# Loads and swaps paced by twos, another model of instruction fetches, and another order, in a planned one-core kernel

## The chip, the cores and the metric

The kernel runs on one core of one Trainium2 chip. Its time is device microseconds (us) of one execution. Before the change it takes 639.13 us, the median of three runs that lie between 637.85 and 642.98 us.

## The reference

Two residual blocks over x of 2048 rows and 512 columns, each modulated by a conditioning vector c. The first is a long convolution with a kernel K that is made from complex exponentials, the second a feed-forward layer with a squared ReLU.

```python
mod = (_silu(c) @ w_mod).reshape(c.shape[0], 6, 1, -1)
sa, ca, ga, sb, cb, gb = (mod[:, 0], ..., mod[:, 5])
h = _layernorm(x) * (1 + ca) + sa
x = x + ga * _A_ref(h, ...)          # K = Re sum_n C exp(dt A l) dt B, then FFT convolution, + u * Dskip
h = _layernorm(x) * (1 + cb) + sb
x = x + gb * _B_ref(h, ...)          # r = relu(h @ w1 + b1); r * r @ w2 + b2, F = 1792
```

## The kernel before, in words

The convolution is done with transforms written as matrix products, in float32. The 512 channels are cut into 8 chunks (letters A to H), and the work is made of **pieces**:

- **rows** (L657 to L667, letter r): each of 16 tiles of x is normalised, turned by PE (L661, L664) into a bank of PSUM, and copied by ACT (L667) into `big`. There are three such banks (`ps`), used in turn.
- **u pieces** (A to H): stage 1 of the transform (L701, copied by ACT at L703) and stage 2 (L711, copied at L735). The stage 1 of any chunk needs all 16 rows.
- **swap** (0 to 7): two DMAs within SBUF (L742) that exchange the two halves of the 128 partitions of a chunk's spectrum, 512 KB each.
- **K units**, 32 of them: POOL adds a phase (L795) and makes amplitudes (L815, L819), ACT takes the sines of the phase (L805 to L807), DVE multiplies (L829 to L832), PE sums (L839), and K goes through stage 1 as well (L701 from `ksb`).
- **products** (a to h): stage 2 of K, the product with the spectrum and the swapped spectrum (L849), the sums (L857) and a copy to `big` (L863).
- **l**: the late modulation, that is sb, cb and gb (L621, L687). **x**: tables of exponentials on ACT (L786). **w**: eight loads of w1 (L933).

Then comes the inverse transform (L1024) with the constants `i2c` (2 MB, L965) and x again (`xt`, L984 and L1040), the second normalisation, transposes (L1064), and the feed-forward layer: three products for each (L1115 to L1118 and L1149 to L1151), with high and low parts of w1 (L977, L996) and of w2 (loads L1084, parts L973 and L974).

`ORDER`, a string, says after which K unit each piece is recorded. It does not fix the order on the engines: `keep_order` does. It takes all recorded instructions in groups, their dependencies and a cost for each, plays the program with one queue for each engine, takes at each step the ready group with the longest way to the end (plus an offset from `HURRY`), and ties each group to the one before it on its engine. So what stands in a row on an engine is a result of that play, and every engine works strictly in that row. On SP the play takes, of the DMAs that are ready, the one recorded first.

The play counts the instructions that PE has taken, in portions (`PACKET`), and delays PE when a portion would come late behind queued DMAs. These delays change only which group the planner picks; the chip fetches its instructions as it does.

Each DMA on SP signals one of eight semaphores in turn, so that the ninth waits for the first. Otherwise SP issues a DMA as soon as its data and its destination are free.

## Time and profile before

| | us |
|---|---|
| median of three runs | 639.13 |
| the profiled execution's own time | 637.81 |
| its span, first to last instruction | 636.0 |
| PE busy | 590.5 |
| DVE, ACT, POOL busy | 371.0, 349.6, 297.4 |

The span is 1.8 us shorter than the time of the same execution, and that execution is 1.3 us below the median. PE is TensorE, DVE VectorE, ACT ScalarE, POOL GpSimd, SP the engine that only issues DMAs. A row of the timeline gives start, duration, engine, line, operation, names (out<-in), shape and count, and in brackets how long the engine was idle before and what ended that. A float32 product stands twice in the trace, so that 16 products of the order are x32 there. "issue" means that the profile shows nothing for which the engine waited. PEclk is the granted clock of PE, 1.00 in full. In a DMA row, q1 is the queue of SP's transfers and q8 that of PE's instruction fetches: packets, MB, share of 16 DMA engines' time.

### The profile page before, as it was taken

Reading aid. Unit: us, or ns where it says so; the run is one execution under the profiler, and the core shown is the slowest. Engines: PE = TensorE matmul, PEld = TensorE weight load, DVE = VectorE, ACT = ScalarE, POOL = GpSimd, SP = SyncE. Lnnn points to the kernel's source line nnn. Section 1 sums busy time; section 2 is a strip of 40 time slices with the busy share of each in tenths; the row PEclk is TensorE's granted clock in tenths of the full one; section 3 lists DMA queues with packets and bytes.
Section 4 is the critical chain, followed back from the end, with each engine's and each line's share of the span. In section 5 each row is a group of like instructions: output and inputs, shape, how many; then the busy total and the mean of one; then the engine's idle time right before and its main releaser. Section 6 shows DMA issues by size and latency. Waiting matters only on the chain.

```text
span 636.0 us, 21183 instructions
## 1 busy us (share of the span) xinstructions
PE 590.5 (93%) x9474; PEld 510.4 (80%) x9474; DVE 371.0 (58%) x652; ACT 349.6 (55%) x651; POOL 297.4 (47%) x247
## 2 busy tenths in 40 slices
PE   1697897999999999898989999999999999999995
PEld 1476797999998899897868888888888888888884
DVE  6886978899799688546655332533325332252223
ACT  5957899889987948362856432253323433222220
POOL 6499699999999987039958100010000100000000
PEclk9999999999999999899999999999999999999999
DMA  8942014022132403662333000100001000010001
GB/s 319 392 140 68 3 35 105 19 55 45 29 70 69 120 4 86 185 250 88 95 110 99 1 1 0 67 0 2 0 1 66 1 1 0 1 66 1 0 1 66
DMA packets 21707, 42.33 MB, mean 67 GB/s; under 512 B 3696, under 2 KB 9200, under 8 KB 20336
## 3 DMA queue, kind: packets, MB, share of 16 engines
q1 hardware_dynamic: 21184, 40.84, 21.0%
q8 instruction: 74, 1.21, 0.8%
q10 hardware_dynamic: 432, 0.14, 0.1%
q14 instruction: 17, 0.14, 0.1%
HBM read 28.39 MB, written 4.19 MB: 51 GB/s over the span
## 4 chain that ended last, share of the span: by engine, by line
PE 72%; ACT 9%; POOL 7%; DVE 5%; issue 4%; DMA 2%; DVEq 0%; SPq 0%; ACTq 0%; POOLq 0%
PE tg L1149 8%; PE tg L1151 8%; PE tg L1150 8%; PE ps L711 7%; PE ps L1115 6%; PE ps L701 6%; PE ps L1116 6%; PE ps L1118 6%; PE ps L857 6%; PE kg L839 3%; PE kg L1115 2%; PE kg L1116 2%; PE kg L1118 2%; PE tg L1024 1%; ACT xy L703 1%
## 5 line engine op out<-in xcount | busy, mean ns | idle before, releaser
L1135 ACT ACTIVATE xy<-ps,b1c 128x512 f32<-128x512 f32 x42 | 29.0, 690 | 126.2 <-PE ps L1118 126.2
L1137 DVE SCALAR_TENSOR_TENSOR ps<-ps,b1c,xy 128x512 f32<-128x512 f32 x42 | 31.8, 758 | 111.1 <-ACT xy L1135 111.1
L1060 POOL TENSOR_TENSOR big<-big,lo 128x512 f32<-128x512 f32 x12 | 15.7, 1306 | 151.8 <-DVE xy L1057 151.8
L711 PE MATMUL ps<-xy,t_sb 128*64 128x64 f32 x2048 | 67.4, 223 | 3.7 <-issue 2.5
L711 PEld LDWEIGHTS ps<-xy,t_sb 128*64 128x64 f32 x2048 | 63.9, 138 | 6.3 <-issue 3.0
L857 PE MATMUL ps<-e_sb,xy 128*64 128x128 f32 (+2 forms) x1152 | 64.2, 270 | 1.9 <-ACT xy L703 1.0
L857 PEld LDWEIGHTS ps<-e_sb,xy 128*64 128x64 f32 x1152 | 59.9, 142 | 3.6 <-ACT xy L703 1.4
L819 POOL TENSOR_TENSOR rtl<-tables 128x1024 f32<-128x1024 f32 x22 | 43.4, 1972 | 0.1
L703 ACT COPY xy<-ps 128x512 f32<-128x512 f32 x64 | 37.0, 598 | 7.7 <-PE ps L701 7.4
L849 DVE TENSOR_TENSOR xy<-ps,xy 128x512 f32<-128x512 f32 x64 | 39.9, 682 | 1.3 <-PE ps L711 1.1
L1115 PE MATMUL ps<-h0h,w1h 128*128 128x512 f32 (+1 forms) x96 | 36.0, 381 | 0.0
L795 POOL TENSOR_TENSOR rtl<-lo,big 128x1024 int32<-128x1024 int32 x16 | 34.3, 2145 | 3.1 <-ACT tg L807 2.5
L701 PE MATMUL ps<-d_sb,big 128*64 128x128 f32 x512 | 32.7, 275 | 2.9 <-ACT big L667 1.4
L701 PE MATMUL ps<-d_sb,ksb 128*64 128x128 f32 x512 | 34.3, 279 | 0.5 <-ACT xy L703 0.4
L863 DVE COPY big<-ps 128x256 f32<-128x256 f32 (+1 forms) x66 | 24.2, 407 | 18.0 <-PE ps L857 17.8
L795 POOL TENSOR_TENSOR llph<-lo,big 128x1024 int32<-128x1024 int32 x16 | 34.5, 2159 | 0.2 <-ACT tg L807 0.2
L701 PEld LDWEIGHTS ps<-d_sb,big 128*64 128x64 f32 x512 | 28.1, 137 | 4.3 <-ACT big L667 1.7
L1115 PE MATMUL ps<-h,w1h 128*128 128x512 f32 x80 | 31.4, 393 | 0.0
L1135 ACT ACTIVATE xy<-kg,b1c 128x512 f32<-128x512 f32 x14 | 9.7, 690 | 39.5 <-PE kg L1118 39.5
L1137 DVE SCALAR_TENSOR_TENSOR kg<-kg,b1c,xy 128x512 f32<-128x512 f32 x14 | 10.6, 756 | 34.0 <-ACT xy L1135 34.0
L701 PEld LDWEIGHTS ps<-d_sb,ksb 128*64 128x64 f32 x512 | 28.8, 140 | 1.6 <-ACT xy L703 0.7
L839 PE MATMUL kg<-rtl 128*32 128x64 f32 x1408 | 25.5, 221 | 4.3 <-issue 3.1
(287 smaller groups left out, 1606.7 us busy)
## 6 DMA issues: line engine op xcount, KB each, us to landing
xy<-xt SPq DMA_DIRECT2D x32, 256.0 KB, 5.5
xy<-xy SPq DMA_DIRECT2D x16, 512.0 KB, 6.0
xy<-w_mod SPq DMA_DIRECT2D x6, 1024.0 KB, 9.2
out_dram<-xy SPq DMA_DIRECT2D x16, 256.0 KB, 2.1
xy<-w SPq DMA_DIRECT2D x14, 256.0 KB, 2.7
raw<-w SPq DMA_DIRECT2D x6, 512.0 KB, 5.3
t_sb<-c_t SPq DMA_DIRECT2D x1, 2048.0 KB, 10.9
i2c<-c_i SPq DMA_DIRECT2D x1, 2048.0 KB, 9.9
```

Of the source, the lines that this page charges most:

```text
L701: nc.tensor.matmul(ps[64 * r : 64 * r + 64, 128 * i : 128 * i + 128], src[:, i], d1_sb[:, r], start=True, stop=True)
L711: nc.tensor.matmul(ps[64 * r : 64 * r + 64, 64 * i : 64 * i + 64].rearrange("p (h q t) -> p q h t", h=2, t=2), t2_sb[:, 8 * g + i, r], src ...
L795: nc.gpsimd.tensor_tensor(ph.rearrange("p d r (a b) -> p (d r) a b", a=4), bc(low_phase[:, us].rearrange("p d r b -> p (d r) b"), 2, 4), b ...
L819: nc.gpsimd.tensor_mul(am[:, 0, :, 32:96].rearrange("p d (v x) -> p d v x", v=2), bc(et[:, 256 + 8 * d0 : 384 + 8 * d0].rearrange("p (y a) ...
L839: nc.tensor.matmul(kps[32 * q : 32 * q + 32, d, :], am[:, r, 4 * q + d, 64:96], am[:, r, 4 * q + d, 0:64], start=(r == 0), stop=(r == 1))
L857: nc.tensor.matmul(ps[64 * m : 64 * m + 64], pairs(y)[:, g, i // 2, 64 * m : 64 * m + 64, i % 2], e1_sb[:, h].rearrange("p (r j) -> p r j" ...
L1115: pe.append(nc.tensor.matmul(ps, w1h[:, q, fs], hh[:, q, cols], start=(q == 0), stop=False))
L1116: pe.append(nc.tensor.matmul(ps, wl[:, q], hh[:, q, cols], start=False, stop=False))
L1118: pe.append(nc.tensor.matmul(ps, w1h[:, q, fs], hl[:, q, cols], start=False, stop=(q == 3)))
L1149: pe.append(nc.tensor.matmul(acc, r2l[:, ms], hi_, start=(t == 0), stop=False))
L1150: pe.append(nc.tensor.matmul(acc, r2h[:, ms], lo_, start=False, stop=False))
L1151: pe.append(nc.tensor.matmul(acc, r2h[:, ms], hi_, start=False, stop=(t == NF - 1)))
```

## The change

1. `paced_load` issues a DMA and remembers it. From the third on, each gets a wait on the landing of the one two places before it (`PACED = 2`, `tc.add_manual_dep` in `keep_order`). It takes the place of the plain issue for the swaps, the w1 loads, `i2c`, the 16 late loads of x and the 14 loads of w2. Both DMAs of one swap remain back to back.
2. `i2c` is loaded in four DMAs of 512 KB. It is recorded ahead of the `xt` loads, as before, and the chain of waits now keeps that order, which before gave way where `i2c` was not ready.
3. The planner's model of instruction fetches has other numbers.
4. `ORDER` and `HURRY` hold other values, and so the planner makes another order.

```diff
+PACED = 2
-HURRY = (176674, 61960, 2605, 274089, 54201, -67055, -175605, 69371)
+HURRY = (392742, 14341, 1606, 250122, 75315, -221787, -342862, -308)
...
-    "rrrrrrrrrrrrrrrrCABCBCBlCBCBACBBA.AA.CAABA.xx.0Caaaa.a.aD1aa..bDbbbEE.DD.bDD2bEb.b.cDDEcccc.cxcc"
+    "rrrrrrrrrxrrxrrrrrCABCBCBCCBCAABB.BCAA.AA.BAl0.aCaaaaa.a.D1..abbbbD2EEx.DDbbDD.E.Dbb.EcDcccc.ccF"
...
+def within(ins):
+    return not any("Dram" in type(a.bass_ap.tensor).__name__.title() for a in (*ins.ins, *ins.outs))
...
+    wait = mybir.DependencyInfo(mybir.DependencyClass.Sync, mybir.DependencyReason.DATA)
     for x, y in behind:
-        before[group[x]].add(group[y])
+        before[group[y.name]].add(group[x.name])
+        tc.add_manual_dep(y, x.name, wait, reason="pace")
...
-                    fetched = max(asked[0] + asked[1], min(behind_ns - 1800, asked[0] + 4300)) + 2350
-                asked = (max(t, fetched), 1100 if fetched > t else 600)
+                    fetched = max(asked[0] + asked[1], min(behind_ns, asked[0] + 4500)) + 2400
+                asked = (max(t, fetched), 1100 if fetched > t else 750)
...
-            queued.append((now, landed))
+            queued.append((now, landed + (-1000 if within(groups[g][0]) else -300)))
...
+    def paced_load(to, of):
+        ins = nc.sync.dma_start(to, of).ins
+        if len(paced) >= PACED:
+            behind.append((paced[-PACED], ins))
+        paced.append(ins)
...
-            nc.sync.dma_start(sw[64 * h : 64 * h + 64], xs[64 - 64 * h : 128 - 64 * h])
+            paced_load(sw[64 * h : 64 * h + 64], xs[64 - 64 * h : 128 - 64 * h])
...
-    nc.sync.dma_start(i2c, c_i2.rearrange("p (j r a) -> p j r a", j=64, r=2))
+    for j in range(0, 64, 16):
+        paced_load(i2c[:, j : j + 16], c_i2.rearrange("p (j r a) -> p j r a", j=64, r=2)[:, j : j + 16])
```

In the changed kernel the lines are shifted: L805 is L818, L667 is L680, L795 is L808, L701 is L714, L711 is L724, L839 is L852, L621 is L634, L687 is L700, and every paced load has the line of the helper, L591.

**ACT at the end of the rows.** L667/L680 are the last copies of the rows, L703/L716 the first copy of stage 1, L805/L818 the sine of a unit's phase and L806/L819 its absolute value; `llph` is the buffer of the second unit. Before:

```order
L535 ACTIVATE big_83<-big_83,magic 128x4x64
L544 ACTIVATE big_83<-big_83 128x4x64
L545 ACTIVATE big_83<-big_83 128x4x64
L667 COPY big_84<-ps_159 128x128x4
L536 ACTIVATE big_83<-big_83,magic 128x4x64
L537 ACTIVATE big_83<-big_83,unmagic 128x4x64
L667 COPY big_84<-ps_157 128x128x4
L667 COPY big_84<-ps_158 128x128x4
L703 COPY xy_97<-ps_159 128x512
```

Now:

```order
L542 ACTIVATE big_83<-big_83,magic 128x4x64
L680 COPY big_84<-ps_158 128x128x4
L543 ACTIVATE big_83<-big_83,unmagic 128x4x64
L818 ACTIVATE tg_425<-llph 128x1024
L680 COPY big_84<-ps_159 128x128x4
L819 ACTIVATE llph<-llph 128x1024
L680 COPY big_84<-ps_157 128x128x4
L680 COPY big_84<-ps_158 128x128x4
L716 COPY xy_97<-ps_159 128x512
```

The second unit's sine, which before stood behind seven copies of stage 1, now stands ahead of the last three copies of the rows. The first unit's sine moved as well, from behind the tenth of the 16 row copies to behind the seventh.

**POOL before the first phase.** L599 and L600 make the scale of four rows, L568 and L771 prepare the phases, L795 is the phase of the first unit. Before:

```order
L568 TENSOR_TENSOR big_83<-big_83 128x4x128 x3
L599 TENSOR_SCALAR mv_71<-mv_71 128x4
L600 TENSOR_TENSOR mv_71<-mv_71,small 128x4
L527 TENSOR_TENSOR big_83<-big_83 128x4x64
L529 TENSOR_TENSOR big_83<-big_83 128x4x64
L771 TENSOR_TENSOR lo<-lo,big_83 128x128x2 x3
L795 TENSOR_TENSOR rtl<-lo,big_83 128x1024
```

Now:

```order
L533 TENSOR_TENSOR big_83<-big_83 128x4x64
L535 TENSOR_TENSOR big_83<-big_83 128x4x64
L574 TENSOR_TENSOR big_83<-big_83 128x4x128 x3
L784 TENSOR_TENSOR lo<-lo,big_83 128x128x2 x3
L808 TENSOR_TENSOR rtl<-lo,big_83 128x1024
L612 TENSOR_SCALAR mv_71<-mv_71 128x4
L613 TENSOR_TENSOR mv_71<-mv_71,small 128x4
```

The last scale of the rows moved behind the first unit's phase. The phase of the second unit follows in both orders after the same instructions.

**PE from the seventh stage 1 to the first unit of K.** L701/L714 is stage 1, L711/L724 stage 2, L621/L634 the late modulation with its transposes L687/L700, L839/L852 the first unit of K. Before:

```order
L701 MATMUL ps_159<-d_sb,big_84 64x128 x8
L621 MATMUL ps_157<-xy_95,srep 32x128 x16
L621 MATMUL ps_159<-xy_96,srep 32x128 x16
L687 MATMUL ps_158<-ident,mt_834 128x128
L701 MATMUL ps_159<-d_sb,big_84 64x128 x8
L687 MATMUL ps_157<-ident,mt_834 128x128
L621 MATMUL ps_158<-xy_93,srep 32x128 x16
L701 MATMUL ps_157<-d_sb,big_84 64x128 x8
L711 MATMUL ps_158<-xy_97,t_sb 64x16x2x2 x16
L839 MATMUL kg_362<-rtl 32x64 x32
```

Now:

```order
L714 MATMUL ps_159<-d_sb,big_84 64x128 x8
L714 MATMUL ps_157<-d_sb,big_84 64x128 x8
L724 MATMUL ps_158<-xy_97,t_sb 64x16x2x2 x16
L714 MATMUL ps_159<-d_sb,big_84 64x128 x8
L724 MATMUL ps_157<-xy_97,t_sb 64x16x2x2 x16
L714 MATMUL ps_158<-d_sb,big_84 64x128 x8
L714 MATMUL ps_159<-d_sb,big_84 64x128 x8
L852 MATMUL kg_362<-rtl 32x64 x32
```

The late modulation moved behind the fourth and fifth unit of K; two stage 1 and one stage 2 more stand ahead of the first unit.

**SP from the second half of w1 to the loads of w2.** `raw11` is that half, `i2c` the constants of the inverse transform, `xy<-xy` swap 7. Before:

```order
L1168 DMA lo_383<-b2 128x512
L933 DMA raw11_4458<-w1 128x4x256 x2
L933 DMA raw11_4458<-w1 128x4x128
L933 DMA raw11_4458<-w1 128x4x256
L742 DMA xy6_97<-xy3_94 64x2048 x2
L984 DMA xy5_96<-xt 128x512 x2
L965 DMA i2c_4572<-c_i2 128x4096
L984 DMA xy4_95<-xt 128x512 x4
L984 DMA xy5_96<-xt 128x512 x2
L1084 DMA xy3_94<-w2 128x512 x7
```

Now:

```order
L1182 DMA lo_383<-b2 128x512
L591 DMA raw11_4395<-w1 128x4x256 x2
L591 DMA xy6_97<-xy1_92 64x2048 x2
L591 DMA raw11_4395<-w1 128x4x128
L591 DMA raw11_4395<-w1 128x4x256
L591 DMA i2c_4572<-c_i2 128x1024 x4
L591 DMA xy2_93<-xt 128x512 x4
L591 DMA xy3_94<-xt 128x512 x4
L591 DMA xy1_92<-w2 128x512 x5
```

Swap 7 moved between the two halves of the w1 loads, and no load of x stands ahead of `i2c` any more.

More of the change, by code (lines that the diff above doesn't have):

```diff
@@ L42 @@
 ON_DVE = {}
-HURRY = (176674, 61960, 2605, 274089, 54201, -67055, -175605, 69371)
+PACED = 2
+HURRY = (392742, 14341, 1606, 250122, 75315, -221787, -342862, -308)
 EXPS = [(0, 1), (1, 1), (2, 2), (4, 2), (6, 2)]
 ORDER = (
-    "rrrrrrrrrrrrrrrrCABCBCBlCBCBACBBA.AA.CAABA.xx.0Caaaa.a.aD1aa..bDbbbEE.DD.bDD2bEb.b.cDDEcccc.cxcc"
-    "F3..EF.EEdddd.FFEd.GF4Fd.d.deGeeFeG.GGFx.HH.G.5HeeeeffGffGfww.6H..Hff.fH.gHHgggw.g.w7.hwghwhghgw"
-    "w"
+    "rrrrrrrrrxrrxrrrrrCABCBCBCCBCAABB.BCAA.AA.BAl0.aCaaaaa.a.D1..abbbbD2EEx.DDbbDD.E.Dbb.EcDcccc.ccF"
+    ".E.FE3c.dxEdddEd.FFd.FdFG.d4.eGeGee.GFFG.HeHe5e..HwefGfGffG.Hf.HH.6ff.fwwg.Hg.wg.Hggww7.ggwhwhhh"
+    "g"
 ).split(".")
@@ L112, in weight @@
     if "DMA" in type(ins).__name__:
-        inside = not any("Dram" in type(a.bass_ap.tensor).__name__.title() for a in (*ins.ins, *ins.outs))
-        return 60, n * out.ap[0][1] * 4 / (180 if inside else 360)
+        return 60, n * out.ap[0][1] * 4 / (180 if within(ins) else 360)
     match str(ins.engine).split(".")[-1]:
@@ L580, in parameters @@
         yield
-    urgent, behind = {}, []
+    urgent, behind, paced = {}, [], []
+    def paced_load(to, of):
[3 more added lines that the diff above has]
+        paced.append(ins)
     def hurry(start, ns):
@@ L932, in load_pieces @@
                 raw1.append(held(kp, f"k0{h}", f"raw1{h}", [P, 4, 896]))
-            nc.sync.dma_start(raw1[h][:, :, f - 896 * h : f - 896 * h + n], w1v[:, :, f : f + n])
+            paced_load(raw1[h][:, :, f - 896 * h : f - 896 * h + n], w1v[:, :, f : f + n])
             yield
@@ L983, in tile_adaln_ssm_ffn @@
     for s in range(8):
-        nc.sync.dma_start(xts[s], xt[s])
+        paced_load(xts[s], xt[s])
     w1la = held(ka, slots[na], "w1la", [P, 4, 512], FR)
@@ L1039, in inverse @@
                 if s + 4 < 16:
-                    nc.sync.dma_start(xts[s + 4], xt[s + 4])
+                    paced_load(xts[s + 4], xt[s + 4])
     def statistics(s):
@@ L1083, in w2_split @@
             hi_, lo_ = t[:, 1024 * i : 1024 * i + 512], t[:, 1024 * i + 512 : 1024 * i + 1024]
-            nc.sync.dma_start(wst, w2v[:, len(w2s)])
+            paced_load(wst, w2v[:, len(w2s)])
             split(hi_, lo_, wst)
```

## The prediction, on record before the run

> **What bounds the kernel now.** I read the page first, for the busy shares, and then the table of windows, with the stages cut where the work on PE changes: loads and rows, first transforms, full K production (two windows), the passage to the feed-forward layer (two), the layer, the last stores.
>
> ```profile
> PE 590.5 (93%) x9474; PEld 510.4 (80%) x9474; DVE 371.0 (58%) x652; ACT 349.6 (55%) x651; POOL 297.4 (47%) x247
> ...
> 0.00:56.80 56.80, 34.62 (x640) 24.86 (x640) 41.10 (x101) 39.40 (x129) 40.71 (x60) 0.97 0.73 257
> 56.80:108.00 51.20, 44.55 (x1306) 40.96 (x1308) 44.67 (x66) 45.93 (x80) 45.85 (x36) 1.00 0.17 37
> 108.00:197.90 89.90, 88.22 (x2558) 84.04 (x2552) 79.65 (x129) 81.36 (x135) 88.88 (x66) 1.00 0.20 43
> 197.90:262.10 64.20, 62.88 (x1850) 60.20 (x1851) 54.78 (x89) 45.02 (x64) 50.54 (x36) 1.00 0.36 98
> 262.10:306.10 44.00, 38.68 (x1132) 34.78 (x1130) 22.20 (x62) 18.87 (x33) 25.43 (x17) 0.92 0.47 153
> 306.10:330.00 23.90, 22.22 (x654) 18.20 (x655) 14.95 (x37) 16.17 (x36) 16.30 (x13) 1.00 0.43 125
> 330.00:629.30 299.30, 299.30 (x1343) 247.42 (x1341) 110.06 (x168) 102.88 (x179) 29.72 (x23) 1.00 0.05 16
> ```
>
> A window row gives length, busy time of PE, PEld, DVE, ACT, POOL, then PEclk, DMA share and GB/s. From 330.00 to 629.30 PE is busy without a gap; the change leaves that work alone, so those 299.3 us and the 6.7 us behind them stay. What can move is PE's idle time ahead of 330: 22.2 us in the first window, 6.7, 1.7, 1.3, 5.3 and 1.7 in the others, and the time in which PE has less than its full clock. In the third window POOL (88.9 of 89.9 us) is as full as PE: there an earlier start of K's production can carry through, and time cannot be made up.
>
> Next the list of PE's waits. I quote those that end with "issue", that is with nothing that another engine or a transfer of the program did: in all 9.4 us.
>
> ```profile
> PE kg L839 <- issue: 3.1, 3, 2.3
> PE ps L711 <- issue: 2.5, 4, 1.4
> PE tg L1024 <- issue: 1.8, 2, 1.1
> PE ps L1064 <- issue: 1.4, 1, 1.4
> PE ps L701 <- issue: 0.6, 1, 0.6
> ```
>
> The longest, 2.28 us, stands in the middle of one unit's products. Here is its place in the timeline, three windows of 4 us around it, and the DMA view of 255.6 to 261.8 us:
>
> ```profile
> 251.66 1.09 PE L701 MATMUL ps<-d_sb,ksb 128*64 128x128 f32 x16
> ...
> 264.39 0.92 PE L839 MATMUL kg<-rtl 128*32 128x64 f32 x38 [2.28 <-issue]
> 265.24 1.98 PE L701 MATMUL ps<-d_sb,ksb 128*64 128x128 f32 x16
> 267.00 2.61 PE L857 MATMUL ps<-e_sb,xy 128*64 128x128 f32 x32
> ...
> 273.17 1.97 PE L857 MATMUL ps<-e_sb,xy 128*64 128x128 f32 x32
> ```
>
> ```profile
> 256.00:260.00 4.00, 4.00 (x130) 4.00 (x128) 3.41 (x7) 2.62 (x5) 0.00 (x0) 1.00 0.96 301
> 260.00:264.00 4.00, 2.11 (x80) 1.88 (x75) 3.40 (x6) 0.00 (x0) 0.00 (x0) 1.00 0.62 176
> 264.00:268.00 4.00, 3.61 (x64) 3.44 (x65) 0.17 (x1) 0.96 (x2) 0.00 (x0) 0.62 1.00 219
> ```
>
> ```profile
> q1 hardware_dynamic: 2055, 1.79, 94.2%
> ```
>
> For 6.2 us the queue of SP's transfers fills 94.2% of the DMA engines with 1.79 MB, the second half of w1 issued at once, and that view has no row of instruction fetches at all. From 108 to 197.9 us there are 20:
>
> ```profile
> q8 instruction: 20, 0.33, 1.5%
> ```
>
> That is one fetch of 16 KB in 4.5 us. So I read the wait as PE having used up its instructions while the next ones stood behind the four loads. It costs more than its 2.28 us: behind it PEclk is 0.62, the 16 products of L701 take 1.98 us for 1.09, and 32 of L857 take 2.61 for 1.97, 1.5 us more.
>
> **The change part by part: w1 by twos.** The waits beside the two groups of w1 loads are the 2.28 us of L839 and the 0.6 of L701; with the 1.5 us of lower clock that is 4.4 us. Two loads are 1.05 MB, at 1.79 MB in 6.2 us an estimated 3.6 us of queue for 6.2: 2.6 us less than a fetch could wait, and the wait was 2.28. That is the case for a gain of the whole 4.4. Against it, the pair of swap 7 (two times 512 KB within SBUF) now stands between the pairs of w1, so two transfers are still queued there. Bounds 0 and 4.4; I take 2.7, nearer the upper, since four in a row don't occur any more.
>
> [...]
>
> **Swaps.** A swap's two halves each wait for those of the swap before.
>
> ```profile
> 92.16 91.49 SPq L742 DMA_DIRECT2D xy<-xy  x10
> ...
> xy<-xy SPq DMA_DIRECT2D x16, 512.0 KB, 6.0
> ```
>
> Ten halves in 91.5 us are one pair in about 23 us, each half landed after 6.0: the wait added is over long before, and both halves still go out together. I count nothing, and leave the 2.5 us of L711 and the rest of L839. Those of L1024 and L1064 (3.2 us) lie where the inverse transform uses up instructions fast; they stay too. The cost if I am wrong on these is in the first rival.
>
> **The start.** Here the order decides.
>
> ```profile
> 27.08 1.28 DVE L595 BATCH_NORM_STATS2 st<-xy 128x6 f32<-128x512 f32 x2
> ...
> 30.46 0.37 DVE L596 BATCH_NORM_AGGREGATE mv<-st 128x2 f32<-128x6 f32 x4
> ```
>
> ```profile
> 30.92 0.23 POOL L599 TENSOR_SCALAR mv<-mv 128x4 f32<-128x4 f32 x1 [6.50 <-DVE mv L596]
> ...
> 55.50 2.31 POOL L795 TENSOR_TENSOR llph<-lo,big 128x1024 int32<-128x1024 int32 x1
> ```
>
> ```profile
> 49.11 1.03 ACT L805 ACTIVATE tg<-rtl 128x1024 f32<-128x1024 int32 x1 [3.47 <-POOL rtl L795]
> 50.08 0.58 ACT L667 COPY big<-ps 128x512 f32<-128x512 f32 x1
> ...
> 55.70 1.05 ACT L667 COPY big<-ps 128x512 f32<-128x512 f32 x2
> ```
>
> ```profile
> 56.81 6.33 PE L701 MATMUL ps<-d_sb,big 128*64 128x128 f32 x112 [1.43 <-ACT big L667]
> 63.07 1.95 PE L621 MATMUL ps<-xy,srep 128*32 128x128 f32 x64
> 64.96 0.33 PE L687 MATMUL ps<-ident,mt 128*128 128x128 f32 x1
> ...
> 67.82 1.08 PE L621 MATMUL ps<-xy,srep 128*32 128x128 f32 x32 [0.36 <-DVE sbc L688]
> ...
> 70.58 1.15 PE L711 MATMUL ps<-xy,t_sb 128*64 128x64 f32 x32 [0.65 <-ACT xy L703]
> 72.92 1.12 PE L839 MATMUL kg<-rtl 128*32 128x64 f32 x64 [1.20 <-DVE rtl L832]
> ```
>
> On POOL the same instructions precede the second unit's phase in both orders. It ended at 57.8. DVE now makes the third group's statistics (L596) right behind L595, at 28.4 for 30.5, so that POOL's 6.50 us of idleness shrinks by about 2 and the phase ends at 55.8 (bounds 51.3 with all of it gone, 57.8 with none). Behind it on ACT, ahead of PE's first stage 1, now stand a sine, a copy, an absolute value and two copies: 0.97 us from start to start (49.11 to 50.08), 0.58, about 1.0 (of the sine's shape) and 1.05, in all 3.6 us. Stage 1 starts at 59.4 (no earlier than the 56.8 that the rows themselves need; at most 61.4) instead of 56.81: 2.6 us later. With 1.43 + 2.6 PE idles longer than in the 2.28 us that cost it 1.5 us of clock, so I add 1.5.
>
> From there to the first unit of K the PE row now has 11 stage 1 (6.33 us for 7) and two stage 2 (1.15 each), 12.2 us in all: the unit comes at 59.4 + 12.2 + 1.5 = 73.1, for 72.92. Ahead of it stand two stage 1 and one stage 2 more than before, 2.95 us, and three modulations and two transposes less, 1.95 + 1.08 + 0.66 = 3.7: PE owes 0.75 us, in a stretch where it has less idle time to hide it. The start is thus +0.9 us. Bounds: with stage 1 at 56.8 and the full clock 69.0, but the product of DVE (L832) that releases the unit has a chain of its own, and as POOL's phase gains 2 I let it gain 2: −2 + 0.75 = −1.2; with 61.4, +2.2 + 0.75 = +2.9.
>
> **The passage.**
>
> ```profile
> 275.63 0.37 SPq L965 DMA_DIRECT2D i2c<-c_i  x1
> ```
>
> ```profile
> 271.04 0.18 POOL L964 COPY i2c<-xy 128x1 f32<-128x1 f32 x1 [16.17 <-DMA xy<-xy]
> ```
>
> `i2c` was free at 271.2, when POOL had seen swap 7 land, and waited on SP until 275.63 behind two loads of x. Now these stand behind it. That gives about 4 us of slack, and swap 7, which the PE row now releases three pieces later (about 1.1 each), takes 3. Behind the waiting loads on SP stand only other loads; the first that anybody needs are those of x, for the sums after the first inverse products. I count 0, from 0 to +3.
>
> The sum on the profiled execution: 637.8 − 2.7 + 0.9 + 0 = 636.0 us. The median lies 1.3 above that execution: **637.3 us** for the median after.
>
> **The rivals.** *All fetch waits go.* If one pair in flight never empties PE's store, 9.4 us and the 1.5 of clock go: 639.1 − 10.9 = 628.2. For it: five lines with the same mark. Against: those at 290 to 324 us lie in windows with a DMA share of 0.4 or less, and the swaps are not thinned. Chance 0.14; with the forecast's own tail below 632.7, faster by over 1% has 0.21.
>
> *Rows wait for K's phase.* Slower, by one mechanism: ACT stands at the second unit's sine with three row copies behind it. It decides once that phase ends after 57.8, where POOL gains nothing: L568, ahead of it, waits for DVE's shifts, and these now stand behind more rows. With an end at 60.0 stage 1 starts at 63.6; PE, idle for 8 us, works two stretches at half clock (3.0); the unit comes at 78.8, 5.9 late, and with the 0.75 owed and no gain on fetches the median is 645.8. For it: ACT waited 3.47 us for POOL in the same stage already. Against: POOL has 6.50 us of idleness ahead. Chance 0.16.
>
> *Pacing does nothing for fetches.* If a fetch waits its turn by packets and not behind the queue, two in flight hold it like four; the start's +0.9 remains: 640.0. Chance 0.20. [...] The 6.2 us without a fetch beside 94.2% speak against it. *The change does not do what it says* for the swaps; that is in the sum.
>
> **How the numbers follow.** 0.50 for the forecast (its own range 632.5 to 642), 0.14, 0.16 and 0.20. About 1% is what a measurement of this kernel can tell from no change: 632.7 to 645.5. Faster: 0.14 + 0.07 of the forecast. Slower: 0.12 of the second rival and 0.03 of others. The rest is within. The range goes from 628 to 645.5, which leaves out about 0.06 below and 0.14 above.
>
> **What would show it.** Right: no "issue" wait over 1 us of L839 near the second half of w1, and PEclk 1.00 there; the first L714 on PE near 59, the first L852 near 73; `i2c` issued within 1 us of POOL's copy. Wrong: "issue" waits of the same sum; the first L714 later than 62; a PE wait for a transfer of x or `i2c` between 280 and 310 us.

## The result and the profile after

The changed kernel takes 636.12 us (median of 10 runs, 632.64 to 639.59), the kernel before 640.44 (637.49 to 643.65) on the same chip: a ratio of 0.9936, 95% interval 0.991 to 0.9961. It is 0.64% faster, within the 1% that the prediction gave as what a measurement of this kernel can tell from no change. Run again, later, it came to 636.76 and 0.9938 (0.9915 to 0.9961). The profiled execution has a span of 634.1 us and took 635.91, that of before 636.0 and 637.81.

The page's busy line and the table of windows, with the cuts of before as far as 306; the last two cuts follow the point from which PE works without a gap (the first product of L1149, now L1163), which comes at 327.4 instead of 329.4:

```profile
PE 592.4 (93%) x9474; PEld 512.9 (81%) x9474; DVE 369.1 (58%) x652; ACT 349.2 (55%) x651; POOL 297.7 (47%) x247
...
0.00:56.80 56.80, 34.79 (x640) 24.98 (x640) 42.39 (x103) 38.26 (x127) 42.69 (x61) 1.00 0.68 239
56.80:108.00 51.20, 45.63 (x1304) 42.46 (x1306) 41.30 (x64) 45.97 (x80) 43.51 (x34) 0.97 0.22 54
108.00:197.90 89.90, 88.62 (x2543) 85.12 (x2541) 78.39 (x129) 80.25 (x136) 88.95 (x67) 1.00 0.20 45
197.90:262.10 64.20, 62.61 (x1910) 59.80 (x1901) 55.68 (x89) 47.35 (x68) 50.80 (x36) 1.00 0.33 86
262.10:306.10 44.00, 40.84 (x1182) 36.08 (x1177) 23.90 (x64) 19.76 (x35) 24.18 (x15) 0.87 0.56 159
306.10:328.00 21.90, 20.52 (x582) 17.00 (x581) 11.88 (x26) 13.94 (x30) 16.24 (x13) 0.95 0.32 88
```

PE's idle time ahead of that point, the lengths of these rows less their busy times, went from 38.8 us to 35.0; the fifth window has 2.2 us less of it and the second 1.1. PE's busy time rose by 1.9 us, with the same 9474 products: PEclk in the fifth window is 0.87, where it was 0.92. So 3.9 us less waiting, 1.9 us given back to a lower clock, 2.0 us in all between these two executions: the gapless stretch began at 327.44 for 329.43.

In the list of PE's waits, those on "issue" are down from 9.4 us to 4.2:

```profile
PE tg L1038 <- issue: 1.8, 3, 0.8
...
PE kg L852 <- issue: 1.2, 1, 1.2
...
PE ps L870 <- issue: 0.6, 1, 0.6
...
PE ps L724 <- issue: 0.4, 1, 0.4
...
PE ps L714 <- issue: 0.2, 1, 0.2
```

A second execution of the same kernel (e1 below) has 6.1 us of them, so part of this drop belongs to the one execution.

The wait of 2.28 us beside the second half of w1 (L839, now L852) is 1.22, and the lower clock behind it is gone: the 16 products of L714 at 262.81 take 1.05 us.

```profile
259.19 0.86 PE L852 MATMUL kg<-rtl 128*32 128x64 f32 x41
261.26 0.64 PE L852 MATMUL kg<-rtl 128*32 128x64 f32 x23 [1.22 <-issue]
261.83 1.15 PE L724 MATMUL ps<-xy,t_sb 128*64 128x64 f32 x32
262.81 1.05 PE L714 MATMUL ps<-d_sb,ksb 128*64 128x128 f32 x16
```

What gave the clock away again stands further back, in the passage. Four windows of the changed kernel, PEclk being the third number from the end:

```profile
292.00:296.00 4.00, 2.36 (x51) 1.38 (x40) 3.90 (x16) 1.87 (x4) 3.62 (x4) 0.82 0.59 189
296.00:300.00 4.00, 3.22 (x150) 2.41 (x154) 3.48 (x13) 3.47 (x9) 1.56 (x2) 0.50 0.48 137
300.00:304.00 4.00, 4.00 (x140) 2.67 (x111) 1.88 (x4) 1.57 (x4) 2.50 (x2) 0.50 0.23 74
304.00:308.00 4.00, 4.00 (x22) 4.00 (x20) 0.84 (x3) 3.90 (x9) 0.17 (x1) 0.50 0.20 66
```

**A common ruler.** The orders differ, so equal instructions can't be compared by their times. For the experiments I use PE's own work instead: each PE instruction is given a fixed weight, an estimate of mine (62.5 ns a product of stage 1, 30.2 of stage 2, 16.4 in K, 44.5 a sum of L870, 14.6 one of the inverse transform, 155 a transpose), these are added up in PE's order, and the table gives how much earlier than in the profiled execution of before a run reached the same sum. Positive is ahead; about 0.5 us is its accuracy, since the orders take up different kinds of work at different times. (At full clock 112 products of stage 1 took 6.33 us, 32 of stage 2 1.15 and 64 in K 1.12 in the kernel before, 128 of the inverse transform 1.91 and four transposes 0.66 in the changed one. The traces give nearer 57 ns for a product of stage 1 and 52 for a sum; with these no entry moves by more than 0.3 us.) The last row needs no ruler: it compares the start of the gapless stretch, since in every run the same products stand ahead of it and no gap behind.

```
before   after  after  no     hold   joined | all    w1     late   parted held   late
reached         again  waits  (e4)   (e7)   | waits  waits  waits  (e8)   (e9)   by 4
at (us)                (e2)                 | (e3)   (e5)   (e6)                 (e12)
104.0    -0.8   -2.5   -1.4   -0.7   -2.5   | -1.1    0.0   -1.0    0.0   +0.3   +0.5
168.5    -0.2   -1.9   -0.7    0.0   -1.9   | -1.0   +0.1   -0.9   +0.1   +0.3   +0.6
206.9    +0.4   -1.3   -0.2   +0.6   -1.2   | -1.0   +0.2   -0.9   +0.1   +0.3   +0.6
258.7    +2.2   +0.4   +1.4   +1.5   +0.3   | -0.3   +0.4   -0.3   -1.4   +1.1   +1.3
276.2    +4.9   +3.0   +4.3   +4.9   +2.6   | +2.9   +4.2   -1.4   +3.3   +4.1   +4.9
287.1    +4.2   +2.3   +3.7   +4.2   +0.8   | +2.8   +4.0   -1.4   +3.3   +4.1   +4.9
303.3    +5.8   +2.2   +3.7   +4.0    0.0   | -0.1   +3.3   -3.8   +1.5   +3.7   +5.7
312.1    +1.7   +0.9   -0.1   +3.4   -1.0   | -3.8   +3.4   -8.7   +1.9   +3.6   +4.7
329.4    +2.0   +1.9   -0.1    0.0   -0.8   | -3.3   +3.4   -8.7   +2.4    0.0   +4.8
```

Left of the bar stand kernels with the new order, right of it kernels with the old one. The first column tells the change in one execution: 0.8 us behind after the start, 2.4 gained between 168 and 259 us, 2.7 more beside the second half of w1 (258.7 to 276.2), and 2.9 lost again in the passage. These are single executions, and not median ones: that of before is 2.6 us below its median, those of e2 and e3 are the slowest of their runs, that of e12 the fastest. Up to 104 us, where no experiment on the old order had changed any row, its executions differ by 1.6 us (-1.1 to +0.5).

### The profile page after: what moved, and what is told of

It is laid out like the page before. It is cut to its first block, busy times and chain, and to the rows that moved or that the text cites. A ratio compares the mean times of both kernels' runs of the same rounds, so it can differ in the third digit from the quotient of the medians.

```text
span 634.1 us, 21191 instructions
## 1 busy us (share of the span) xinstructions
PE 592.4 (93%) x9474; PEld 512.9 (81%) x9474; DVE 369.1 (58%) x652; ACT 349.2 (55%) x651; POOL 297.7 (47%) x247
## 4 chain that ended last, share of the span: by engine, by line
PE 67%; POOL 17%; DVE 6%; ACT 5%; issue 4%; DMA 1%; DVEq 0%; POOLq 0%; ACTq 0%
PE tg L1163 8%; PE tg L1164 8%; PE tg L1165 8%; PE ps L1129 6%; PE ps L1130 6%; PE ps L1132 6%; PE ps L870 4%; PE ps L714 4%; PE ps L724 4%; POOL rtl L832 3%; POOL rtl L808 3%; POOL llph L808 3%; PE tg L1038 2%; PE kg L1129 2%; PE kg L1130 2%
## 5 line engine op out<-in xcount | busy, mean ns | idle before, releaser
L1149 ACT ACTIVATE xy<-ps,b1c 128x512 f32<-128x512 f32 x42 | 29.0, 691 | 125.6 <-PE ps L1132 125.6
L724 PE MATMUL ps<-xy,t_sb 128*64 128x64 f32 x2048 | 67.5, 223 | 2.4 <-ACT xy L716 1.9
L724 PEld LDWEIGHTS ps<-xy,t_sb 128*64 128x64 f32 x2048 | 64.2, 138 | 4.9 <-ACT xy L716 2.7
L870 PE MATMUL ps<-e_sb,xy 128*64 128x128 f32 (+2 forms) x1152 | 62.8, 265 | 0.7 <-issue 0.6
L870 PEld LDWEIGHTS ps<-e_sb,xy 128*64 128x64 f32 x1152 | 58.5, 139 | 2.5 <-issue 1.0
L716 ACT COPY xy<-ps 128x512 f32<-128x512 f32 x64 | 37.2, 593 | 13.9 <-PE ps L714 12.0
L714 PE MATMUL ps<-d_sb,big 128*64 128x128 f32 x512 | 32.9, 281 | 3.8 <-ACT big L680 3.6
L808 POOL TENSOR_TENSOR rtl<-lo,big 128x1024 int32<-128x1024 int32 x16 | 34.3, 2144 | 4.0 <-DVE big L876 3.4
L714 PE MATMUL ps<-d_sb,ksb 128*64 128x128 f32 x512 | 34.3, 275 | 1.1 <-DVE mt L698 0.6
L808 POOL TENSOR_TENSOR llph<-lo,big 128x1024 int32<-128x1024 int32 x16 | 34.3, 2146 | 0.1
L714 PEld LDWEIGHTS ps<-d_sb,big 128*64 128x64 f32 x512 | 29.5, 142 | 4.6 <-ACT big L680 3.8
L1149 ACT ACTIVATE xy<-kg,b1c 128x512 f32<-128x512 f32 x14 | 9.6, 688 | 37.7 <-PE kg L1132 37.7
L714 PEld LDWEIGHTS ps<-d_sb,ksb 128*64 128x64 f32 x512 | 27.9, 137 | 2.2 <-DVE mt L698 0.8
L843 DVE TENSOR_TENSOR rtl<-rtl,tg 128x1024 f32<-128x1024 f32 x22 | 26.7, 1212 | 3.5 <-POOL rtl L832 3.5
```

The costliest lines, as they stand in the source:

```text
L714: nc.tensor.matmul(ps[64 * r : 64 * r + 64, 128 * i : 128 * i + 128], src[:, i], d1_sb[:, r], start=True, stop=True)
L724: nc.tensor.matmul(ps[64 * r : 64 * r + 64, 64 * i : 64 * i + 64].rearrange("p (h q t) -> p q h t", h=2, t=2), t2_sb[:, 8 * g + i, r], src ...
L808: nc.gpsimd.tensor_tensor(ph.rearrange("p d r (a b) -> p (d r) a b", a=4), bc(low_phase[:, us].rearrange("p d r b -> p (d r) b"), 2, 4), b ...
L870: nc.tensor.matmul(ps[64 * m : 64 * m + 64], pairs(y)[:, g, i // 2, 64 * m : 64 * m + 64, i % 2], e1_sb[:, h].rearrange("p (r j) -> p r j" ...
```

## The experiments

The lines in a diff are those of the kernel that it starts from. Medians, ratios and intervals go by the runs of the kernel before on the same chip (640.25, 640.43, 639.09 and 640.37 us in the four groups: e1 to e4, e5 to e8, e9 to e11, e12).

**e1, the changed kernel again.** No edit.

> The changed kernel once more, as the measure for the other runs of this study. If the four windows at half clock between 294 and 308 us come from the order (short fetch waits among the 32x32 products of the inverse transform), they are there again, PEclk about 0.5 over at least 10 us of 290 to 312. If they were chance of that one execution, PEclk is 1.00 there with at most one window at half clock. Time 636 us either way, 0.991 to 0.997 of the kernel before.

636.76 us. The same program, but another passage:

```profile
292.00:296.00 4.00, 3.49 (x142) 2.82 (x138) 3.90 (x15) 1.29 (x3) 3.46 (x4) 1.00 0.57 173
296.00:300.00 4.00, 2.75 (x72) 2.14 (x73) 2.68 (x9) 0.97 (x2) 2.35 (x2) 0.69 0.42 126
300.00:304.00 4.00, 3.55 (x195) 2.84 (x164) 3.52 (x12) 3.70 (x10) 1.28 (x1) 0.88 0.43 123
304.00:308.00 4.00, 2.98 (x80) 2.25 (x78) 2.26 (x6) 2.68 (x7) 2.49 (x2) 1.00 0.18 44
```

One window at half clock (3.4 us), not four (13.7). The four windows are not the order's. In this execution the time went elsewhere: two windows at half clock at the start (2.5 us behind at 104), and longer issue waits among the products of the inverse transform (4.0 us in all, for 1.8). Both reach the gapless stretch at 327.4 to 327.5 us. A single profile of this kernel thus says little on one or two microseconds of the passage or the start; what follows rests on medians, and on places where several executions agree.

**e2, the new order without the waits.** PE, ACT, DVE, POOL and SP have the same instructions in the same order as the changed kernel.

```
-        tc.add_manual_dep(y, x.name, wait, reason="pace")
```

> The changed order, instruction for instruction on every engine, but no transfer waits for the one two places before it. Theory (instruction fetches stand behind queued loads): the wait of PE on issue in the K unit beside the second half of w1 returns from 1.2 us to over 2, a window at half clock follows it, and the sum of issue waits before the FFN rises from 4 us by 2 or more: 638.5 to 640 us. Rival (the order alone brought the gain): the sum of issue waits stays within 1 us of the changed kernel's and the time at 636.

635.29 us, 0.9928 (0.99 to 0.9957): the theory fell. The wait beside the second half of w1 is 0.92 us, less than with the waits, and the sum of all waits on issue is 6.0 us, for 4.2 and 6.1 in the two executions with waits:

```profile
260.05 0.86 PE L851 MATMUL kg<-rtl 128*32 128x64 f32 x41
261.83 0.64 PE L851 MATMUL kg<-rtl 128*32 128x64 f32 x23 [0.92 <-issue]
```

The new order does not need them. The trace suggests a reason, which e7 and e8 test: swap 7 stands between the halves of that group in SP's row, and has to wait for its own input, so the last two loads go out at 265.5 and 267.4 us, where in the kernel before they went at 255.9 and 257.4, whether they wait for a landing or not.

**e3, the waits without the new order.** The old order on all engines; each of the same transfers waits for the one two before it in SP's row.

```
+            if ins.name in paced:
+                if len(issued) >= 2:
+                    tc.add_manual_dep(ins, issued[-2], wait, reason="pace")
+                issued.append(ins.name)
```

> The old order, instruction for instruction, with the waits alone: each of the same transfers (swaps, w1, i2c in one piece, late x, w2) waits for the one two places before it in SP's row. Theory: the 2.28 us of L839 at 264 falls to 1.2 or less and the half clock behind it goes; about 2.7 us less than the kernel before, 637.7. Rival (waits do nothing): the 2.28 us stays within 0.5, time as before, 640.4.

638.93 us, 0.9988 (0.997 to 1.0006), between the two forecasts. The table shows both theories at work. Beside w1 the run gains 3.2 us (from -0.3 to +2.9), and L839's wait of 2.28 us is 0.58. Then it loses 6.2 in the passage (this execution is the slowest of its twelve). In the list of waits two stand there, of which the kernel before had 0.3 us of the first and nothing of the second:

```profile
PE ps L1072 <- ACT xy L1063: 3.0, 1, 3.0
...
PE kg L1072 <- ACT xy L1063: 1.8, 1, 1.8
```

L1072 is a transpose of normalised rows (L1064 before), L1063 ACT's normalisation. So e5 and e6 part the waits.

**e4, large products kept for the passage** (new order). The last group of sums is held until the first transposes.

```
+        if s == 0:
+            held_back.append((pe[0].ins.name, last_sums[3]))
```

> The changed kernel, but the last group of sums of the last channel group (L870, 16 products, 1.4 us) is held until the first block of transposes of the normalised rows is through, so that PE has it while the second block waits for ACT, and works on large products between the 32x32 ones. Theory (short waits among the 32x32 products put PE's clock to half, and 32x32 products alone do not bring it back): at most two windows at half clock instead of four between 290 and 310 us, 2.5 to 4.5 us less than the changed kernel, 632 to 633.5. Rival (the windows come by chance, or from something before 290 us): as many as in the changed kernel, 636 us, or up to 1 us more for the sums that come later.

639.45 us, 0.9994 (0.9969 to 1.0018), slower than the changed kernel by more than its interval. There are two windows at half clock between 290 and 315, as many as the theory allowed, though e1 without the edit has one; and still it lost: with sums that come later, the first product of the gapless stretch waits 2.3 us for ACT (1.03 before), and another wait on issue of 1.57 us appears at 311.7. Fewer windows at half clock were no gain by themselves here.

**e5, waits on w1 alone** (old order), and **e11**, the same again.

```
-            nc.sync.dma_start(raw1[h][:, :, f - 896 * h : f - 896 * h + n], w1v[:, :, f : f + n])
+            paced_load(raw1[h][:, :, f - 896 * h : f - 896 * h + n], w1v[:, :, f : f + n])
```

> The old order, instruction for instruction; only the eight loads of w1 wait, each for the one two before it. Theory (the waits cure the fetch beside w1, worth about 3 us, and the later waits on x, i2c and w2 gave it back in the run with all waits): the wait of L839 at 264 falls below 1.2 us, the passage from 290 to 330 us is as in the kernel before, 637 to 637.7 us. Rival (the gain beside w1 is given back whatever comes after it): within 1 us of the run with all waits, 639.

635.66 us, 0.9943 (0.9911 to 0.9975): eight waits in the old order bring what the whole change brings. The unit beside w1:

```profile
261.08 0.64 PE L847 MATMUL kg<-rtl 128*32 128x64 f32 x26
262.00 0.83 PE L847 MATMUL kg<-rtl 128*32 128x64 f32 x38 [0.28 <-issue]
262.76 1.09 PE L709 MATMUL ps<-d_sb,ksb 128*64 128x128 f32 x16
```

0.28 us for 2.28, and full clock behind it. The time is lower than the 637 to 637.7 that were expected.

> The old order with waits on the eight loads of w1 alone, once more, on the chip of the other two: 635 to 637 us, 0.991 to 0.9965 of the kernel before. In its passage an instruction fetch had waited 2.7 us behind i2c and the loads of x that go out at once; if that is the rule and not chance, a wait on issue of over 1.5 us stands between 285 and 292 us again.

635.76 us, 0.9954 (0.9929 to 0.998). The 2.71 us that a product of the inverse transform waited at 288.5 in e5, with 6.1 us between two fetches while `i2c` and the loads of x landed, did not return: 0.38 us at 287.3. Another wait of 1.66 us on issue stands at 294.9, with 3.7 us between the fetches and nothing queued. It stands behind 128 products of the inverse transform that took 1.91 us (291.12) and the first of a block of transposes; that they used up instructions faster than the fetches came is my estimate from these times.

**e6, waits on the late loads alone** (old order): `i2c`, the late x and w2.

```
-    nc.sync.dma_start(i2c, c_i2.rearrange("p (j r a) -> p j r a", j=64, r=2))
+    paced_load(i2c, c_i2.rearrange("p (j r a) -> p j r a", j=64, r=2))
```

and likewise at `xts` and `wst`.

> The old order, instruction for instruction; only i2c, the late loads of x and those of w2 wait, each for the one two before it. Theory (these loads then land later, ACT stands at its first split of w2 with the normalisation behind it, and PE waits for its transposes): the 2.28 us beside w1 stay, PE waits over 2 us for ACT at its first transposes near 298, w2's first load lands 4 us or more later than the 290.07 of the kernel before: 642 to 645 us. Rival (late loads have slack): 640, as the kernel before.

645.72 us, 1.0071 (1.0046 to 1.0097). This is the loss. ACT's first split of w2 in the kernel before, then ACT's row in this run, and PE's first transposes:

```profile
290.15 1.21 ACT L973 CAST w<-xy 128x512 fp32r<-128x512 f32 x2 [7.82 <-DMA xy<-w]
```

```profile
299.22 1.22 ACT L981 CAST w<-xy 128x512 fp32r<-128x512 f32 x2 [15.52 <-DMA xy<-w]
300.35 0.29 ACT L1054 ACTIVATE rstd<-mv,epsb 128x1 f32<-128x1 f32 x1
301.12 0.81 ACT L1063 ACTIVATE xy<-big,mv,rstd 128x512 f32<-128x512 f32 x1 [0.48 <-DVE mv L1061]
```

```profile
301.98 1.11 PE L1072 MATMUL ps<-ident,xy 128*128 128x128 f32 x4 [3.17 <-ACT xy L1063]
...
305.55 0.66 PE L1072 MATMUL ps<-ident,xy 128*128 128x128 f32 x4
```

The x loads now go out in twos, the loads of w2 stand behind them on SP, and the first lands at 299.1 us where it landed at 290.1. ACT went through its row in order: it stood at the split of w2 (15.52 us, for 7.82), and the normalisation that PE's transposes need, behind it in the row, came at 301.12 us. The old order puts that split ahead of the normalisation, the new one behind the fourth tile's (at 300.90 us); that may be why the same waits cost the new order nothing that shows (e1 against e2). e9 and e10 test it. At w1, left as it was, the wait was 2.94 us, and another 2.29 stood beside the swap.

**e7, the new order with w1's second half joined** (no waits). Only SP's row differs: the last two loads of w1 stand ahead of swap 7.

```
+    late = [ins for ins in sp if ins.name in w[6:]]
+    sp[at:] = late + [ins for ins in sp[at:] if ins not in late]
```

> The changed order without its waits, every engine's row the same but SP's: there the last two loads of w1 stand ahead of swap 7 again, right behind the two before them, so that four loads are queued at once as in the kernel before. Theory (it is the swap's place between the halves of w1 that thins the queue in the new order): PE's wait on issue beside them is over 2 us where the run without waits had 0.9, and a window at half clock follows; 638 to 639.5 us. Rival (the place of the swap does not matter, other moves of the order do it): wait below 1.3, 635 to 636.5 us.

638.13 us, 0.9952 (0.9928 to 0.9976). The wait is 1.38 us and a second of 0.39 follows, for 0.92 in e2: the theory's direction, but not its 2 us, no window at half clock behind it, and the intervals of e2 and e7 overlap. In the new order the place of the swap accounts for part of the gain at most: with neither waits nor the swap between the loads, e7 still gains 2.3 us beside w1 (0.3 to 2.6 in the table, for 2.9 in e2). Which other move of the order brings these stays open.

**e8, the old order with w1's second half parted** (no waits). Again only SP's row differs: swap 7 stands ahead of the last two loads.

```
+    sp[:] = [ins for ins in sp if ins not in late]
+    sp[at:at] = late
```

> The old order without any wait added, every engine's row the same but SP's: there swap 7 stands ahead of the last two loads of w1, so that these go out about 8 us later. Theory (as above): the 2.28 us of L839 at 264 falls below 1.2, no half clock behind it, and the passage stays: 637 to 638 us. Rival: the 2.28 us stays within 0.5, 640 us; or w1's last loads come too late for ACT's casts and PE waits for them, 641 or more.

637.08 us, 0.9951 (0.9927 to 0.9975). There is no wait left in that unit, and what follows it runs at full clock:

```profile
262.90 1.24 PE L847 MATMUL kg<-rtl 128*32 128x64 f32 x64
264.07 1.09 PE L709 MATMUL ps<-d_sb,ksb 128*64 128x128 f32 x16
```

The table has the largest step of all there, 4.7 us (from -1.4 to +3.3); but a wait of 1.33 us on issue at 219.9, which no other execution has, had put this one behind, and from 206.9 us on it gains 3.2. By the medians the place of one pair of transfers is worth about as much in the old order as the eight waits of e5. Later two waits on issue of 1.83 and 2.48 us stand in its passage.

**e9 and e10, all waits in the old order, with the splits of w2 held** until the fourth (e9) or the second (e10) row tile is normalised.

```
+        cast = nc.scalar.copy(hi_, raw_).ins.name
+        if normed:
+            held_back.append((normed[3], cast))
```

> The old order with all waits, as in the run that came to 639, but ACT's splits of w2 (L973 of the kernel before) are held until the fourth normalised row tile has been written (L1055). Theory (what the late waits cost is ACT standing at the first split with the normalisation behind it): ACT's 15 us wait for w2 ahead of the normalisation and PE's waits of 2.96 and 1.85 us for ACT at the transposes go, the gain beside w1 is kept, 634 to 636.5 us. Rival (the late x loads themselves hold the sums and so the normalisation): PE still waits 2 us or more at its first transposes, 638 to 640 us.

638.1 us, 0.9985 (0.9959 to 1.001).

> The same, but the splits of w2 are held only until the second normalised row tile has been written. Theory: the first transposes' wait is gone as well; the third and fourth tile may still wait for a split (0.62 us each, or its load): between the run held to the fourth tile and that without holding, 634.5 to 638 us. Rival as there: 638 to 640 us.

638.42 us, 0.9978 (0.9954 to 1.0001). The mechanism is as expected, the time is not. PE's waits for ACT at the transposes went from 2.96 and 1.85 us to 0.91 and none in e9, and at 312 us e9 is 3.6 us ahead where e3 was 3.8 behind. What was late next are the x loads themselves, and then the fetches. DVE's first sum and the wait of PE that follows from it:

```profile
290.75 1.41 DVE L1046 TENSOR_TENSOR big<-xy,tg 128x256 f32<-128x256 f32 x4 [5.38 <-DMA xy<-xt]
```

```profile
291.88 2.10 PE L1037 MATMUL tg<-big,i2c 32*32 32x128 f32 x128 [1.43 <-DVE big L1046]
...
307.43 2.66 PE L1037 MATMUL tg<-big,i2c 32*32 32x128 f32 x183
311.92 0.42 PE L1037 MATMUL tg<-big,i2c 32*32 32x128 f32 x9 [1.83 <-issue]
```

Holding the splits also moved a block of 64 products of the inverse transform forward, so that 192 now follow each other; after 183 of them PE waited 1.83 us on issue, a window at half clock came behind it, and the 3.6 us were gone. In e10 PE's wait for the first sum is 2.48 us, and one of 1.35 on issue stands at 312.7. That these waits alone keep the medians at 638 is argued from one execution each, not shown.

**e12, waits on the late loads by four** (old order; w1 by two as in e5).

```
+                n = paced[ins.name]
+                if len(issued) >= n:
+                    tc.add_manual_dep(ins, issued[-n], wait, reason="pace")
```

> The old order, instruction for instruction; the loads of w1 wait for the one two before, and i2c and the late loads of x and w2 for the one four before. Theory (late loads cost by coming late, and a fetch waits behind as much as is queued): i2c and three loads of x in flight are as much as without waits, so the first load of w2 lands within 2 us of the 286.5 of the run with waits on w1 alone, PE waits no more for ACT, and the fetch at 288 may still wait 1 to 2.7 us: 635 to 637 us, no better than waits on w1 alone. Rival (any wait on the late loads costs, as the 645.7 us of those by two): 640 us or more.

634.2 us, 0.9928 (0.9893 to 0.9962), the lowest median of the study. ACT's wait at the split is 8.98 us, w2's first load has landed at 286.3, and PE's waits for ACT at the transposes are 0.78 and 0.39:

```profile
286.43 1.22 ACT L982 CAST w<-xy 128x512 fp32r<-128x512 f32 x2 [8.98 <-DMA xy<-w]
288.06 0.29 ACT L1055 ACTIVATE rstd<-mv,epsb 128x1 f32<-128x1 f32 x1 [0.42 <-DVE mv L1054]
```

As in e11, a wait on issue (1.70 us at 292.6) stands in the passage, with 3.5 us between two fetches and nothing queued. Between two and four late loads in flight lies the difference between the loss in e3 and e6 (638.93 and 645.72 us) and none that shows. Against the changed kernel (0.9936) and e5 (0.9943) its interval does not separate it: it is as good, with the old order and none of the search. It is one run, and under the 635 to 637 us that were expected.

**The fetch measured.** In each execution I took the two instruction fetches (16 KB, PE's queue) around the wait beside w1's second half: the time from the start of one fetch to the start of the next, PE's wait, and how long after the end of the second fetch's transfer PE went on.

```
                        interval   PE waits   PE goes on after the fetch has landed
e6 late waits           7.02       2.94       1.46
before                  6.27       2.28       1.40
e7 joined               5.72       1.38       1.31
e1 after again          5.47       1.22       1.32
after                   5.42       1.22       1.29
e9 held                 5.32       0.83       1.23
e11 w1 waits again      5.17       0.75       1.26
e2 no waits             5.03       0.92       1.35
e3 all waits            4.70       0.58       1.41
e12 late by four        4.64       0.45       1.45
e5 w1 waits             4.55       0.28       1.39
e10 held early          at most 3.99 there, no wait
e4 hold                 at most 3.91 there, no wait
e8 parted               at most 3.90 there, no wait
```

In every row with a wait PE goes on 1.2 to 1.5 us after a fetch has landed, and it waits what the interval exceeds some 4.0 to 4.5 us by. Counted along PE's row, all these waits stand at one place: behind 6348 products in the old order, 6347 in the new; and where a second wait follows, it stands exactly 128 products on. The same goes for the rest of K's production and the passage: between 76 and 332 us the fourteen executions have 102 waits on "issue" of over 0.25 us, at only 14 places of either order, and each ended 1.1 to 1.6 us after a fetch had landed. So I read these waits on "issue" as waits for the instruction fetch, and the one beside w1 as held up by what is queued: with PE's row there unchanged, the runs of the old order that thin the queue (e3, e5, e8 to e12) have at most 0.83 us of it, the others 2.28 and 2.94 (before, e6). How long it gets is not set by the number of loads alone. The changed kernel's order with the same waits shows 1.22, 1.22 and none (after, e1, e4), and four loads at once gave 2.28, 2.94 and 1.38 (before, e6, e7).

## Why the prediction was right, and where it was not

The forecast was 637.3 us, within 1% of the kernel before; measured were 636.12 and -0.64%. The level was close, the gain was too small: 639.1 to 637.3 is -1.8 us, measured were -4.3 between the medians. Between the two profiled executions the change is -1.9 us, but that of before lay 2.6 us below its median of ten runs; on three runs it had seemed 1.3. That this -1.9 agrees with the sum's -1.8 is luck: 2.4 us that the sum did not have were gained between 168 and 259, and 2.9 that it counted as 0 were lost in the passage.

*w1 by twos, -2.7.* The size is right by luck, for a cause that is half right. Beside the second half the changed kernel gained 2.7 us (2.6, 2.9 in the next two executions of the order), the wait went from 2.28 to 1.22, and PEclk is 1.00. That it would be under 1 us was wrong. The reading, a fetch behind the queue, fits every row above that has a wait: PE went on 1.23 to 1.46 us after a fetch had landed. The step that failed is the one that gave it to the waits "by twos": e2 has the gain without them. And the prediction counted swap 7 between the pairs as the case against, "two transfers are still queued there"; e8 shows that it is worth 3 to 4.7 us in the old order. It had the moved row in front of it and read it as more traffic, not as 8 us between two bursts. In the new order the swap's place is not the whole of it either (e7).

*Swaps, nothing.* Right: e5 leaves them without waits and loses nothing.

*The other issue waits, left as they were ("I count nothing").* For those of the inverse transform and the transposes this held: 3.2 us before, 1.8, 4.0 and 3.9 in the changed kernel, e1 and e2. For those ahead of w1's second half it was wrong, and this is the mis-sized term. Between 168 and 259 us the new order gains 2.4 us (2.3 and 2.1 in e1 and e2). There the kernel before waited 0.57 us on issue at 191, 0.64 and 0.34 at 210 to 214 behind four loads of w1's first half, 0.33 at 236, and 1.0 for ACT at 198; the changed one 0.17 and 0.37. Its w1 loads go out one by one, the first behind swap 5 at 217.7 us, the others behind swap 6 at 240.3, 242.4 and 244.9; no run parts this from the other moves of the order. The prediction had 0.6 us of this in its bound of 4.4 and took 2.7 for both halves.

*The start, +0.9.* Right in its steps: POOL's second phase ended at 56.1 (55.8 forecast, 57.8 before), stage 1 began at 59.66 (59.4), the first unit of K came at 73.97 (73.1), and the kernel is 0.8 us behind at 104 us; e1, e2 and e4, with the same start, are 2.5, 1.4 and 0.7 behind, where the old order's executions lie between 1.1 behind and 0.5 ahead.

*The passage, 0 to +3.* `i2c` went out at 272.58, 0.65 us after POOL's copy began, as said, and no transfer of x or `i2c` held PE. But 2.9 us were lost there in the profiled execution, 4.4 in e2 and 1.1 in e1: there the waits on issue and the windows at half clock stand, and no wait for the loads. The range held the first and the last of these; the reason was not among those given. And one move that the order showed was passed over: the splits of w2 that went behind the normalisation on ACT. By e3, e6 and e9 it takes away PE's waits for ACT. That it is what keeps the waits of the change from costing what they cost in the old order, 5.3 us in e6, is argued and not shown: e9 and e10 held the splits and were not faster than e3 clear of the noise.

*The rivals.* All fetch waits gone (628.2): 4.2 us of 9.4 are left, 6.1 in e1. Rows waiting for K's phase (645.8): the phase came earlier, not later. Pacing does nothing for fetches (640.0): of the waits in the new order that is so, for a reason that this rival did not have; in the old order they do (e5).

## What to carry to other kernels

All 102 waits on "issue" counted here ended 1.1 to 1.6 us after an instruction fetch had landed. Where such a wait stands next to a DMA queue that is full (94.2% beside w1 in the kernel before), look for the fetch's row in the DMA view, and part the bursts, by the place of a transfer in the row or by waits; in the old order one of the two was enough (no wait in e8 and 0.28 us in e5, for 2.28). Limit what is in flight only for transfers that nobody waits for soon: by twos the late loads cost 5.3 us (e6), by fours nothing that shows (e12). In e6 the late load became a wait for what stood behind the instruction that needed it: ACT was idle for 15.52 us at its first split of w2, and PE then for 3.17 us at the transposes whose normalisation came behind that split. Where a change brings a mechanism and a new order together, run each without the other before the gain is put down to the mechanism.

## What the runs showed of the hardware

No two fetches of PE's instructions started less than 3.3 us apart (3.30 in the kernel before, 3.33 in the changed one), in fourteen executions of 74 fetches each. By the counts a fetch of 16 KB brings an estimated 256 instructions, that is 128 products with their weight loads: 74 fetches serve 9474 products and as many weight loads, and the second waits beside w1 stand 128 products behind the first. 128 products of the inverse transform lasted about 2 us (1.91 in the changed kernel, 1.99 and 2.12 in e12), less than the shortest interval between two fetches. That a long row of such products waits for fetches also with nothing queued is an estimate from these times. The waits that go with it: in e9, 183 in a row were followed by 1.83 us; in e11 and e12 1.66 and 1.70 us came with nothing queued, 3.7 and 3.5 us between the fetches.

Ahead of the gapless stretch PE's granted clock was at 0.50 for 3.41 us or four times that: in the kernel before for 3.41 from 29.48, 265.00 and 299.13 us, in the changed one for 3.41 from 59.04 and for 13.65 from 294.56. A window is a stretch of that length here. In the fourteen executions, 18 windows at full clock in the passage (284 to 312 us) in which PE was busy for 0.27 to 0.65 of the time were followed by one at half clock, and four of 0.56 to 0.63 were not. Most of the 18 held 32x32 products; two (0.27 in e10, 0.51 in e11) held none. Between 57 and 284 us, among the other kinds of products, 25 windows had shares of 0.43 to 0.66 and none was followed by one at half clock; the one of 0.33, beside w1 in the kernel before, was. Ahead of 57 us, where PE waits for its first data, windows of up to 0.51 were. In the two executions of the pair the highest share of such a window was 0.65 (2.21 us, from 291.15 in the changed kernel). No share thus parts the windows of one kind from those of the other. What brought the clock back is not settled: behind a window at half clock that PE filled with 32x32 products and transposes the next was at half clock again in the changed kernel (301.4 to 304.8 us), and at full clock in e1 (297.6 to 301.0). Between one and four windows of the passage were at half clock; what decided it in an execution was not settled either.
